# Attention backward on one core: K and V loads moved to the GpSimd queue, dO·O to VectorE, and nearly all K transposes to DMA

## The chip, the cores and the metric

The program runs on one core of one Trainium2 chip. Its engines work side by side, each through its own list of instructions in order: TensorE (PE, with its weight loads as PEld), VectorE (DVE), ScalarE (ACT), GpSimd (POOL) and SyncE (SP). SP does no arithmetic here; it issues DMAs. POOL computes and issues DMAs too, from a queue of its own. The metric is the device time of one execution in microseconds, given as the median of the runs; less is better.

## The reference

Two attention blocks A and B with the same shapes stand side by side. Each projects its input, attends to a cache of keys and values, and projects back; the two outputs are concatenated. The kernel computes the output and, for a given gradient of it, all ten gradients.

```python
B, Sq, D = 8, 96, 640
H, Sk, Dh = 32, 512, 128
def block(x, k_cache, v_cache, wq, wo):            # bfloat16
    q = (x @ wq).reshape(B, Sq, H, Dh).transpose(0, 2, 1, 3)
    s = einsum("bhqd,bhkd->bhqk", q, k_cache) * Dh ** -0.5
    p = softmax(s, axis=-1)
    o = einsum("bhqk,bhkd->bhqd", p, v_cache)
    return o.transpose(0, 2, 1, 3).reshape(B, Sq, H * Dh) @ wo
def forward(...):
    return concatenate([block(A...), block(B...)], axis=-1)
def reference(..., grad_out):
    out, vjp = jax.vjp(forward, A_x, ..., B_wo)
    return out, *vjp(grad_out)
```

## The kernel before

**Tiles and ticks.** One tile is one batch element of one head: 96 queries against 512 keys, with a head dimension of 128. There are 2 blocks x 32 heads x 8 batch elements = 512 tiles. They are worked in a software pipeline whose unit is a tick: tile number n stands at tick `ct = tick0 + h * 8 + b`, and each of its steps is given to an `Emitter` with a tick (`ct` plus an offset from the table `OFF`, line 45) and a slot within the tick (line 51). The emitter sorts by tick and slot and calls the steps (lines 21 to 28). A scheduler may then move instructions against this order. Those in `pinned(...)` (line 111) keep their program order, and those under `tc.high_priority` (the scores and the softmax, lines 291 to 331) move ahead.

**The steps of a tile**, with its tick offset. `c_ld` (line 262) loads K and V of two batch elements at once, 256 KB each: K at -5, V at -3, on SP. `c_xt` (line 272) is a crossbar DMA transpose on SP: VT, the transpose of a V pair, at 0 for all pairs, and KT at -3 for those K pairs that `k_on_pe` (line 548) does not send elsewhere. `c_s1` (line 280), at +2, transposes K on PE into `kT_ps`, four 128-column matmuls against the identity for each tile, and DVE copies the result to `KT_pe`. At +3 the scores follow, `S_ps = Q·KT` (line 298), their row maximum on DVE (`negm`, line 300), the exponential on ACT (`E_sb`, line 310), the reciprocal of the row sum on DVE (`rinv`, line 320), and the scaling on POOL (`P_sb`, line 329). At +4 PE transposes P (line 365) and computes dV (line 389); at +5 it computes O^T from V and P^T (line 359), and `c_s5b` (line 401) forms `prod = dO·O` on POOL. At +6 come dP = dO·VT (line 417), the row sums of `prod` (`dl_ps`, line 419) and dS on DVE (line 421); at +7 dK (line 432) and the transpose of dS (line 346); at +8 dQ^T from K (line 340). ACT evacuates O, dQ, P^T, dV and dK. Stores of dV and dK, two batch elements together (256 KB each), go out on POOL's queue in `c_st` (line 395), pinned, at slot 54.3.

**Where K is transposed before the change.** By line 549 on PE for every other pair of batch elements, for head 0 of both blocks and for head 1 of block A. That makes 268 tiles on PE; the other 244 tiles, 122 pairs, take a DMA.

**Buffers.** The pool `kv` holds 7 K pairs, 5 V pairs, 2 KT pairs and 4 VT pairs (lines 575 to 579). A load or transpose waits until the last reader of its buffer is done. All PSUM tiles share 8 banks.

**Work per head.** Beside its 8 tiles a head has projections and transposes of its own (pB, pC, pD, qA, qB, qD), put at fixed ticks around it. Heads form groups of 5 or 6 (2 at the end of B). When a group ends, `gU` (line 501) multiplies the group's O and dQ with the weights (`o_ps`, line 512), over some 14 to 18 ticks. So there are stretches of heads with this group work on PE and stretches without it.

**Queues.** SP's list in a steady stretch is the loads of K and V and the transposes KT and VT, each behind the waits of the one before. POOL's list in one tick is P_sb, prod, one store, and now and then a load of weights (`wq_p`, `wo_h`, lines 190 and 199) or a store of their gradients (lines 474 and 496).

Of the kernel before, what the change touches and what calls it, by code (L numbers as in the profile page):

```python
# [8 lines left out]
ALU = mybir.AluOpType  # L9
# [32 lines left out]
SL_GRP = 95  # L42
SL_SETUP = 96

OFF = dict(ldk=-5, ldv=-3, kt=-3, vt=0, s2=3, s3=3, s4=4, s5=5, s6=6, s7=7, s8=8)
HK = dict(pA=-10, pA2=-9, pB=-3, pC0=[-2, 0], pC1=[-1, 0], pD1=1, pD0=2, qA0=18, qA1=17, qB=[19, 20], qD=[(18, 0, 2), (19, 2, 4), (21, 4, 5)])
EV = dict(pB0="act", pB1="dve", pC00="act", pC01="act", pC10="act", pC11="dve", pD0="dve", pD1="dve", qA0="act", qA1="dve", qB0="act", qB1="dve", qD="dve", gU="act")
GSPREAD0 = 9
# [2 lines left out]
SLOTS = dict(LOAD=0, S2A=5, S2B=5.5, S1=6, S8=10, S7=20, S5=30, S4=40, S6=50, S3A=52, S3B=53, S5B=54, HEAD=SL_HEAD, GRP=SL_GRP)  # L51


def build_block(tc, em, tick0, blk, x, kc, vc, wq, wo, g_all, out_all, dx, dk, dv, dwq, dwo, ident, ones, pools, HG=6, first=True, groups=None):
    nc = tc.nc
# [7 lines left out]
    KC = Sk // 128  # L63
    NB = 2
# [46 lines left out]
    def pinned(ins):  # L111
        return tc.keep_in_program_order(ins)
# [68 lines left out]
    def pA(h):  # L181
        def f():
            start = first and h == 0
            if h % 2 == 0:
                wq_p = hd.tile([128, DC, 256], BF16, name="wq_p", bufs=2)
                with nc.allow_non_contiguous_dma(reason="wq slice of two heads"):
                    if start:
                        nc.sync.dma_start(wq_p[:], wq_v[:, :, h * 128:(h + 2) * 128])
                    else:
                        pinned(nc.gpsimd.dma_start(wq_p[:], wq_v[:, :, h * 128:(h + 2) * 128]))  # L190
            else:
                wq_p = HS[(blk, h - 1)]["wq_p"]
            HS[(blk, h)] = dict(wq_p=wq_p, wq_h=wq_p[:, :, (h % 2) * 128:(h % 2 + 1) * 128])
        return f

    def pA2(h):
        def f():
            wo_h = hst.tile([128, D], BF16, name="wo_h", bufs=HG + 3)
            ld = nc.gpsimd.dma_start(wo_h[:], wo[h * 128:(h + 1) * 128, :])
            if not (first and h == 0):  # L200
                pinned(ld)
            HS[(blk, h)]["wo_h"] = wo_h
        return f

    def pB(h):
        def f():
            st = HS[(blk, h)]
            woT_ps = bank([128, DC * 128], BF16, "woT_ps")
            for c in range(DC):
                nc.tensor.transpose(woT_ps[:, c * 128:(c + 1) * 128], st["wo_h"][:, c * 128:(c + 1) * 128], ident[:])  # L210
            woT_h = hd.tile([128, DC * 128], BF16, name="woT_h", bufs=1)
            evac(EV["pB0"], woT_h[:], woT_ps[:])
            st["woT_h"] = woT_h
            wqT_ps = bank([128, DC * 128], BF16, "wqT_ps")
            for c in range(DC):
                nc.tensor.transpose(wqT_ps[:, c * 128:(c + 1) * 128], st["wq_h"][:, c, :], ident[:])
            wqT_h = hst.tile([128, D], BF16, name="wqT_h")
            evac(EV["pB1"], wqT_h[:], wqT_ps[:])
            st["wqT_h"] = wqT_h
            st["slot"] = (blk * H + h) % OD.shape[2]  # L220
            st["OT_h"] = OD[:, 0, st["slot"]]
            st["dQT_h"] = OD[:, 1, st["slot"]]
            st["QT_h"] = hd.tile([128, T], BF16, name="QT_h")
            st["dOT_h"] = hd.tile([128, T], BF16, name="dOT_h")
        return f
# [36 lines left out]
    def c_ld(h, b, n, bufs):  # L262
        def f():
            src = kc if n == "K" else vc
            X = kvp.tile([128, NB, KC, 128], BF16, name=n + "_sb", bufs=bufs)
            nc.sync.dma_start(X[:], src[b:b + NB, h].rearrange("b (p c) d -> p b c d", c=KC))
            for i in range(NB):
                st = CS.setdefault((blk, h, b + i), {})
                st[n + "_sb"], st[n + "_all"] = X[:, i], X
        return f  # L270
# [130 lines left out]
    def c_s5b(h, b):  # L401
        def f():
            st = CS[(blk, h, b)]
            hs = HS[(blk, h)]
            tok = slice(b * Sq, (b + 1) * Sq)
            prod = wk.tile([128, Sq], BF16, name="prod", bufs=3)
            pinned(nc.gpsimd.tensor_tensor(prod[:], hs["OT_h"][:, tok], hs["dOT_h"][:, tok], op=ALU.mult))  # L407
            st["prod"] = prod
        return f

# [135 lines left out]
    NTS = len(tsplits)  # L546

    def k_on_pe(h, b):
        return (b // NB) % 2 == 0 or h == 0 or (first and h == 1)

    SX = pools["SX"]
    for g in range(NG):
        h0 = GH0[g]
        for hh in range(groups[g]):
            h = h0 + hh
            c0t = tick0 + h * B
            if not (first and h == 0):
                em.add(c0t + HK["pA"], 54.6, pA(h))
                em.add(c0t + HK["pA2"], 54.6, pA2(h))
            em.add(c0t + HK["pB"], SL_HEAD, pB(h))  # L560
            fh = first and h == 0
            p0, p1, d1, d0, late = HK["pC0"], HK["pC1"], HK["pD1"], HK["pD0"], 0
            if fh:
                p1, d1, d0, late = [3, 3], 3, 4, 7
            elif h == 0:
                p0, p1, d1, d0, late = [-2, 2], [0, 3], 3, 4, 7
            for si in range(NTS):
                em.add(c0t + p0[min(si, 1)], SL_HEAD, pC(h, 0, si))
                em.add(c0t + p1[min(si, 1)], SL_HEAD + late, pC(h, 1, si))
            em.add(c0t + d1, SL_HEAD + (8 if late else 0), pD(h, 1))  # L570
            em.add(c0t + d0, SL_HEAD, pD(h, 0))
            for b in range(B):
                ct = c0t + b
                if b % NB == 0:
                    em.add(tick0 - 12 if first and h == 0 and b == 0 else ct + OFF["ldk"], SLOTS["LOAD"], c_ld(h, b, "K", 7))
                    em.add(ct + OFF["ldv"], SLOTS["LOAD"], c_ld(h, b, "V", 5))
                    if not k_on_pe(h, b):
                        em.add(ct + OFF["kt"], SLOTS["LOAD"] + 1, c_xt(h, b, "KT", 2))
                    em.add(ct + OFF["vt"], SLOTS["LOAD"] + 1, c_xt(h, b, "VT", 4))
                if k_on_pe(h, b):  # L580
                    em.add(ct + 2, SLOTS["S1"], c_s1(h, b))
                em.add(ct + OFF["s2"], SLOTS["S2A"], c_s2a(h, b))
                em.add(ct + OFF["s2"], SLOTS["S2B"], c_s2b(h, b))
                em.add(ct + OFF["s3"], SLOTS["S3A"], c_s3a(h, b))
                em.add(ct + OFF["s3"], SLOTS["S3B"], c_s3b(h, b))
                em.add(ct + OFF["s5"], SLOTS["S5B"], c_s5b(h, b))
                if b % 2 == 1:
                    em.add(ct + OFF["s4"] + 1, 54.3, c_st(h, b, "v"))
                    em.add(ct + OFF["s7"] + 1, 54.3, c_st(h, b, "k"))
                em.add(ct + OFF["s4"], SLOTS["S4"], c_s4(h, b))  # L590
                for i, o in enumerate(("s8", "s7", "s5", "s4")):
                    SX.setdefault(ct + OFF[o], [None] * 4)[i] = (blk, h, b)
                em.add(ct + OFF["s6"], SLOTS["S6"], c_s6(h, b))
                em.add(ct + OFF["s7"], SLOTS["S7"], c_s7(h, b))
            hk = HK if first or h < H - 1 else dict(HK, qA0=13, qB=[14, 15], qA1=16, qD=[(19, 0, 2), (19, 2, 4), (19, 4, 5)])
            em.add(c0t + hk["qA0"], SL_HEAD, qA(h, 0))
            for di in range(len(wsplits)):
                em.add(c0t + hk["qB"][di], SL_HEAD + 1, qB(h, di))
            em.add(c0t + hk["qA1"], SL_HEAD, qA(h, 1))
            for (k_, c_lo, c_hi) in hk["qD"]:  # L600
                if c_lo < DC and h % 2 == 1:
                    em.add(c0t + k_, SL_HEAD + 2, qD(h, c_lo, min(c_hi, DC)))
        cLg = tick0 + (h0 + groups[g] - 1) * B + B - 1
        gs0 = max(3, (GSPREAD0 * groups[g]) // HG)
        gs1 = max(3, (GSPREAD1 * groups[g]) // HG)
        if not first and g == NG - 2:
            gs0, gs1 = 9, 9
        if g == 0:
            em.add(cLg + OFF["s5"] - 2, SL_LOAD, setup_acc)
        subs = [(0, t, gi) for t in range(TT) for gi in range(len(gsplits))] + [(1, t, gi) for t in range(TT) for gi in range(len(gsplits))]  # L610
        n_out = TT * len(gsplits)
        for i, (which, t, gi) in enumerate(subs):
            if which == 0:
                tk = cLg + OFF["s5"] + 2 + (i * gs0) // n_out
            else:
                tk = cLg + OFF["s8"] + 2 + gs0 - 3 + ((i - n_out) * gs1) // n_out
            em.add(tk, SL_GRP, gU(g, which, t, gi))
# [124 lines left out]
```

## Time and profile before

| | |
|---|---|
| median of 3 runs | 1707.16 us (1696.48 to 1713.74) |
| profiled execution, its span | 1699.8 us |
| mean granted TensorE clock | 0.998 |
| PEld, DVE, ACT, POOL busy | 79%, 78%, 83%, 61% of the span |
| DMA | 423.05 MB in 600429 packets, mean 249 GB/s |
| HBM read and written | 161.09 MB and 159.12 MB |

Busy time of an engine is the union of its instructions' spans. Instructions of PE and ACT overlap their followers, so a busy share near 100% on PE means that it is hardly ever empty, not that it is at its peak. The share of a DMA queue is the time of its packets over the time of 16 DMA engines; as packets overlap too, the shares may add up to more than 100%. In a group of instructions, the idle time is that of the engine just before it, with what ended it. The time to landing of a DMA runs from the start of its issue to its last completion.

### The profile page before, as it was taken

Reading aid. Unit: us, or ns where it says so; the run is one execution under the profiler, and the core shown is the slowest. Engines: PE = TensorE matmul, PEld = TensorE weight load, DVE = VectorE, ACT = ScalarE, POOL = GpSimd, SP = SyncE. Lnnn points to the kernel's source line nnn. Section 1 sums busy time; section 2 is a strip of 40 time slices with the busy share of each in tenths; the row PEclk is TensorE's granted clock in tenths of the full one; section 3 lists DMA queues with packets and bytes.
Section 4 is the critical chain, followed back from the end, with each engine's and each line's share of the span. In section 5 each row is a group of like instructions: output and inputs, shape, how many; then the busy total and the mean of one; then the engine's idle time right before and its main releaser. Section 6 shows DMA issues by size and latency. Waiting matters only on the chain.

```text
span 1699.8 us, 56567 instructions
## 1 busy us (share of the span) xinstructions
PE 1675.7 (99%) x22024; PEld 1343.8 (79%) x22024; DVE 1329.8 (78%) x3052; ACT 1405.2 (83%) x3518; POOL 1040.3 (61%) x1747
## 2 busy tenths in 40 slices
PE   8999999999999999999999999999999999999999
PEld 7877778778778778777778877887788778778876
DVE  6887678878788878787778876787788778878877
ACT  6998889869869869878768998897799679878975
POOL 3676567646647647656566764675576557656754
PEclk9999999999999999999999999999999999999999
DMA  9999999999999999999999999999899989999994
GB/s 256 252 259 250 258 225 260 262 242 243 262 221 252 268 238 259 225 251 237 281 256 269 273 270 248 238 289 248 218 261 276 237 221 261 281 217 240 263 247 141
DMA packets 600429, 423.05 MB, mean 249 GB/s; under 512 B 419360, under 2 KB 557984, under 8 KB 600160
## 3 DMA queue, kind: packets, MB, share of 16 engines
q1 hardware_dynamic: 546576, 242.08, 72.2%
q0 software_dynamic: 53584, 177.35, 32.7%
q8 instruction: 173, 2.83, 0.7%
q14 instruction: 96, 0.79, 0.2%
HBM read 161.09 MB, written 159.12 MB: 188 GB/s over the span
## 4 chain that ended last, share of the span: by engine, by line
PE 89%; DMA 4%; ACT 3%; issue 1%; DVE 1%; POOL 0%; SPq 0%; DVEq 0%; ACTq 0%; POOLq 0%
PE q_ps L243 12%; PE o_ps L512 12%; PE dwo_ps L470 6%; PE dV_ps L389 6%; PE dK_ps L432 6%; PE S_ps L298 6%; PE dP_ps L417 6%; PE dwq_ps L490 6%; PE x_ps L340 5%; PE x_ps L365 5%; PE dst_ps L346 5%; PE x_ps L359 5%; PE kT_ps L285 3%; PE n_ps L258 3%; PE nat_ps L455 2%; DMA VT<-V_sb 1%
## 5 line engine op out<-in xcount | busy, mean ns | idle before, releaser
L329 POOL TENSOR_SCALAR P_sb<-E_sb,rinv 96x512 bf16<-96x512 bf16 x512 | 352.6, 689 | 567.8 <-DVE rinv L320 559.2
L310 ACT ACTIVATE E_sb<-S_ps,negm 96x512 bf16<-96x512 f32 x512 | 351.0, 686 | 187.6 <-DVE negm L300 181.9
L421 DVE SCALAR_TENSOR_TENSOR dS_sb<-dP_ps,dl_ps,P_sb 96x512 bf16<-96x512 f32 x512 | 382.1, 746 | 60.9 <-PE dl_ps L419 54.6
L300 DVE TENSOR_REDUCE negm<-S_ps 96x1 f32<-96x512 f32 x512 | 347.6, 679 | 50.9 <-PE S_ps L298 46.6
L435 ACT ACTIVATE dK_sb<-dK_ps 128x512 bf16<-128x512 f32 x512 | 302.1, 590 | 63.4 <-PE dK_ps L432 56.5
L392 ACT ACTIVATE dV_sb<-dV_ps 128x512 bf16<-128x512 f32 x512 | 311.6, 609 | 0.0
L378 ACT ACTIVATE PT_sb<-x_ps 128x384 bf16<-128x384 bf16 x512 | 253.1, 494 | 0.0
L512 PEld LDWEIGHTS <-OD 128*128 128x128 bf16 x1536 | 132.2, 98 | 100.4 <-issue 1.0
L398 POOL DMA_DIRECT2D out_dram<-dV_sb x256 | 194.9, 761 | 11.8 <-issue 8.6
L398 POOL DMA_DIRECT2D out_dram<-dK_sb x256 | 195.0, 762 | 9.1 <-issue 4.4
L389 PE MATMUL dV_ps<-dOnat_h,P_sb 96*128 96x128 bf16 x2048 | 198.2, 219 | 0.8 <-DVE dOnat_h L160 0.6
L417 PE MATMUL dP_ps<-VT,dOT_h 128*96 128x512 bf16 x512 | 195.4, 382 | 3.0 <-DMA VT<-V_sb 3.0
L432 PE MATMUL dK_ps<-Qnat_h,dS_sb 96*128 96x128 bf16 x2048 | 198.1, 219 | 0.1
L407 POOL TENSOR_TENSOR prod<-OD,dOT_h 128x96 bf16<-128x96 bf16 x512 | 184.2, 360 | 13.8 <-ACT OD L375 12.6
L348 DVE COPY dST_sb<-dst_ps 128x384 bf16<-128x384 bf16 x512 | 177.1, 346 | 10.5 <-PE dst_ps L346 10.3
L365 PE MATMUL x_ps<-ident,P_sb 96*128 96x96 bf16 x2048 | 172.0, 205 | 0.8 <-POOL P_sb L329 0.3
L359 PE MATMUL x_ps<-PT_sb,V_sb 128*128 128x96 bf16 x2048 | 172.3, 206 | 0.2 <-ACT PT_sb L378 0.2
L346 PE MATMUL dst_ps<-ident,dS_sb 96*128 96x96 bf16 x2048 | 172.3, 206 | 0.2 <-DVE dS_sb L421 0.2
L340 PE MATMUL x_ps<-dST_sb,K_sb 128*128 128x96 bf16 x2048 | 171.0, 206 | 1.3 <-ACT dK_sb L435 0.8
L375 ACT ACTIVATE OD<-x_ps 128x192 bf16<-128x192 f32 (+1 forms) x515 | 167.9, 326 | 3.9 <-PE x_ps L340 3.9
L320 DVE RECIPROCAL rinv<-rowsum 96x1 f32<-96x1 f32 x512 | 79.9, 156 | 106.0 <-ACT E_sb L310 100.4
L340 PEld LDWEIGHTS <-K_sb 128*128 128x128 bf16 x2048 | 131.1, 98 | 25.1 <-issue 1.6
(84 smaller groups left out, 3744.4 us busy)
## 6 DMA issues: line engine op xcount, KB each, us to landing
out_dram<-dV_sb POOLq DMA_DIRECT2D x256, 256.0 KB, 5.2
out_dram<-dK_sb POOLq DMA_DIRECT2D x256, 256.0 KB, 5.3
K_sb<-in_A_k_cache_dram SPq DMA_DIRECT2D x128, 256.0 KB, 5.3
V_sb<-in_A_v_cache_dram SPq DMA_DIRECT2D x128, 256.0 KB, 5.2
K_sb<-in_B_k_cache_dram SPq DMA_DIRECT2D x128, 256.0 KB, 5.0
V_sb<-in_B_v_cache_dram SPq DMA_DIRECT2D x128, 256.0 KB, 4.9
out_dram<-dwo_sb POOLq DMA_DIRECT2D x63, 160.0 KB, 4.8
out_dram<-dwq_sb POOLq DMA_DIRECT2D x31, 320.0 KB, 6.1
```

The costliest lines, as they stand in the source:

```text
L300: nc.vector.tensor_reduce(negm[:], S_ps[:], axis=AX.X, op=ALU.max, negate=True)
L310: nc.scalar.activation(E_sb[:], st["S_ps"][:], ACT.Exp, bias=st["negm"][:], scale=1.0, accum_out=rowsum[:])
L329: pinned(nc.gpsimd.tensor_scalar(P_sb[:], st["E_sb"][:], st["rinv"][:], 0.0, op0=ALU.mult, op1=ALU.add))
L340: nc.tensor.matmul(dQT_ps, st["K_sb"][:, c, :], st["dST_sb"][:, c * Sq:(c + 1) * Sq], start=(c == 0), stop=(c == KC - 1))
L389: nc.tensor.matmul(dV_ps[:, c * 128:(c + 1) * 128], P_sb[:, c * 128:(c + 1) * 128], hs["dOnat_h"][:, b * 128:(b + 1) * 128], start=True, s ...
L392: nc.scalar.activation(SB[(blk, h, b // 2, "v")][:, b % 2], dV_ps[:], ACT.Identity, scale=1.0)
L398: pinned(nc.gpsimd.dma_start(dst[b - 1:b + 1, h].rearrange("b (p c) d -> p b (c d)", c=KC), SB.pop((blk, h, b // 2, which))[:]))
L417: nc.tensor.matmul(dP_ps[:], hs["dOT_h"][:, tok], st["VT"], start=True, stop=True)
L421: nc.vector.scalar_tensor_tensor(dS_sb[:], dP_ps[:], dl_ps[:, 0:1], st["P_sb"][:], op0=ALU.subtract, op1=ALU.mult)
L432: nc.tensor.matmul(dK_ps[:, c * 128:(c + 1) * 128], dS_sb[:, c * 128:(c + 1) * 128], hs["Qnat_h"][:, b * 128:(b + 1) * 128], start=True, s ...
L435: nc.scalar.activation(SB[(blk, h, b // 2, "k")][:, b % 2], dK_ps[:], ACT.Identity, scale=1.0)
L512: nc.tensor.matmul(o_ps[:], src[:, t * 128:(t + 1) * 128], rhs, start=(hh == 0), stop=(hh == groups[g] - 1))
```

## The change

Four edits, made together:

1. `c_ld` issues all loads of K and V from POOL's queue, pinned, but for head 0 of block A, which stays on SP. Their slot becomes 54.4, behind P_sb (53) and the stores (54.3) of the same tick, instead of 0.
2. V is loaded at tick -4 instead of -3.
3. `prod` is computed on DVE, not pinned, instead of POOL.
4. `k_on_pe` keeps PE transposes of K for head 0 of both blocks and head 1 of block A only. All other K pairs take a DMA transpose. The numbers of buffers stay as they are.

```diff
-OFF = dict(ldk=-5, ldv=-3, kt=-3, vt=0, s2=3, s3=3, s4=4, s5=5, s6=6, s7=7, s8=8)
+OFF = dict(ldk=-5, ldv=-4, kt=-3, vt=0, s2=3, s3=3, s4=4, s5=5, s6=6, s7=7, s8=8)
...
-            nc.sync.dma_start(X[:], src[b:b + NB, h].rearrange("b (p c) d -> p b c d", c=KC))
+            v = src[b:b + NB, h].rearrange("b (p c) d -> p b c d", c=KC)
+            if first and h == 0:
+                nc.sync.dma_start(X[:], v)
+            else:
+                pinned(nc.gpsimd.dma_start(X[:], v))
...
-            pinned(nc.gpsimd.tensor_tensor(prod[:], hs["OT_h"][:, tok], hs["dOT_h"][:, tok], op=ALU.mult))
+            (nc.vector.tensor_tensor(prod[:], hs["OT_h"][:, tok], hs["dOT_h"][:, tok], op=ALU.mult))
...
     def k_on_pe(h, b):
-        return (b // NB) % 2 == 0 or h == 0 or (first and h == 1)
+        return h == 0 or (first and h == 1)
...
-                    em.add(tick0 - 12 if first and h == 0 and b == 0 else ct + OFF["ldk"], SLOTS["LOAD"], c_ld(h, b, "K", 7))
-                    em.add(ct + OFF["ldv"], SLOTS["LOAD"], c_ld(h, b, "V", 5))
+                    sl = SLOTS["LOAD"] if first and h == 0 else 54.4
+                    em.add(tick0 - 12 if first and h == 0 and b == 0 else ct + OFF["ldk"], sl, c_ld(h, b, "K", 7))
+                    em.add(ct + OFF["ldv"], sl, c_ld(h, b, "V", 5))
```

## The prediction

> **What bounds the kernel now.** I read the page first for who is full, then DMA, then two-head stretches, then the orders on the queues. The page's busy times, queues, the GB/s of 40 slices, and the chain:
>
> ```profile
> PE 1675.7 (99%) x22024; PEld 1343.8 (79%) x22024; DVE 1329.8 (78%) x3052; ACT 1405.2 (83%) x3518; POOL 1040.3 (61%) x1747
> ...
> GB/s 256 252 259 250 258 225 260 262 242 243 262 221 252 268 238 259 225 251 237 281 256 269 273 270 248 238 289 248 218 261 276 237 221 261 281 217 240 263 247 141
> ...
> q1 hardware_dynamic: 546576, 242.08, 72.2%
> q0 software_dynamic: 53584, 177.35, 32.7%
> ...
> PE 89%; DMA 4%; ACT 3%; issue 1%; DVE 1%; POOL 0%; SPq 0%; DVEq 0%; ACTq 0%; POOLq 0%
> ```
>
> PE sets the time, but the DMA queues together are at 104.9% of 16 engines' packet time. The mean of these hides two kinds of stretch. In the answer by windows, the 45.2 us rows are two heads without group work ("light"), the others two heads with it ("heavy"); the columns are length, busy time of each engine, PE clock, DMA share, GB/s:
>
> ```profile
> 955.00:1000.20 45.20, 45.13 (x639) 37.81 (x636) 37.92 (x88) 42.72 (x109) 32.19 (x55) 1.00 1.16 267
> 1000.20:1061.10 60.90, 60.90 (x754) 46.49 (x751) 38.77 (x88) 51.14 (x129) 32.49 (x55) 1.00 1.07 260
> 1088.20:1133.40 45.20, 45.14 (x639) 37.81 (x637) 37.91 (x89) 42.73 (x109) 32.20 (x54) 1.00 1.10 274
> 1154.90:1216.40 61.50, 61.21 (x753) 46.61 (x751) 45.90 (x107) 44.45 (x111) 32.42 (x55) 1.00 0.98 237
> 1243.90:1289.10 45.20, 45.13 (x638) 37.81 (x636) 37.91 (x89) 42.72 (x109) 32.16 (x54) 1.00 1.10 263
> ```
>
> The light stretch takes the same 45.2 us each time: PE is bound there, ACT close behind at 42.7. Bytes of one head: loads 8 x 262 KB, stores 8 x 262 KB, transposes 4 VT and on average 2 KT, weights and their gradients 160 + 160 + (320 + 320)/2 KB, together 6.43 MB. Two heads in 45.2 us ask for 285 GB/s, and the windows moved 263 to 274; heavy ones ask for 211 and moved 237 to 260. So I read that DMA already falls behind in light stretches and catches up in heavy ones, unseen by PE because loads run ahead.
>
> **The change part by part.**
>
> *K off PE.* 268 tiles on PE become 24 (heads 0, 0 and 1), so 244 go. Cost of one, from the timeline of a light stretch (start, duration, engine, line):
>
> ```profile
> 1404.13 0.39 PE L285 MATMUL kT_ps<-ident,K_sb 128*128 128x128 bf16 x4
> ...
> 1404.35 0.33 PE L340 MATMUL x_ps<-dST_sb,K_sb 128*128 128x96 bf16 x4
> ```
>
> The next group starts 0.22 us later; the 0.39 is pipelined. 244 x 0.22 = 53.7 us off the path that sets the end (the chain gives line 285 3%, 51 us for 268, which agrees). That is 1.76 us per two heads: light 43.4, heavy about 59.4. With the copies DVE loses 244 x 0.41 = 100 us.
>
> *prod on DVE.* No row shows it there. Nearest from below the reciprocal on 96x1 (156 ns), from above an f32 addition on 128x128 out of PSUM (277 ns); I take 250, as the shape is nearest to the latter: 512 x 0.25 = 128 us (80 to 142). DVE ends near 1358 us, off the path. It waits for ACT's O in front of DVE's later work, but by the timeline that evacuation ends before dS, which precedes prod. A pause there would delay `negm`, on which ACT already waits 181.9 us. Cost 0, bounds -5 to +15.
>
> *Loads on POOL.* 504 of 512 loads move (block A's head 0 stays). The stores of equal size give the price:
>
> ```profile
> L398 POOL DMA_DIRECT2D out_dram<-dV_sb x256 | 194.9, 761 | 11.8 <-issue 8.6
> ...
> L407 POOL TENSOR_TENSOR prod<-OD,dOT_h 128x96 bf16<-128x96 bf16 x512 | 184.2, 360 | 13.8 <-ACT OD L375 12.6
> ```
>
> 504 x 0.761 = 384 us come, 184 us of prod go: POOL 1040 + 200 = 1240 us. In a light stretch 32.2 - 16 x 0.36 + 16 x 0.76 = 38.6 of 43.4 us. Each tick holds P_sb, one store, one load: the move of V to -4 puts K and V in alternate ticks, and costs nothing of its own; the fifth V buffer is free at that tick. Behind a load that waits stand the next P_sb and, for that, PE. A load waits for dQ or O matmuls early in its own tick, which are over, and in the built order each POOL DMA waits for the eighth before it, now 3.4 ticks (9 us) old instead of 7. Stores land in 5.2 us, at most 11.9, so this costs nothing until landing nears 9 us; bounds 0 to 40 us (P_sb up to 0.4 us late in 100 of the light ticks).
>
> On the price of issuing: the Trainium skill, "DMA: Bandwidth & Descriptors", Issuing engines are not separate DMA queues, says that all DMAs interleave on the same 16 engines and that spreading them saves sequencer time only. By that rule the move to POOL gives DMA no capacity, so it speaks against any gain there. The trace has the same work on both queues only at different packet sizes, so it can't confirm it.
>
> *122 more transposes.* 122 x 262 KB = 32 MB, 455 MB in all. SP has room: 504 issues leave. Price in DMA time, two ways.
> By bytes: four light windows (the three above, and one at 255) move 265 GB/s on average. 455 MB / 265 = 1717 us; at the best slice, 289, 1574.
> By packet time: q0 is 556 us for 177.35 MB, 3.13 us per MB; loads at the same price leave q1's 99 MB of transposes 1227 - 143 x 3.13 = 779 us, 2.06 us each. 122 more are 251 us, and the sum is 1783 + 251 = 2034 us of share. At 1.16, the fullest light window, that needs 1753 us; at 1.10, 1849.
> The trace doesn't show transposes beside loads on the software queue, whose packets are larger (177.35 MB in 53584 against 242.08 in 546576), so that the mixture could run better. I take the bytes, as the nearest measured thing, and the packet time for the upper end.
>
> The Trainium skill, "Advanced Engine Details and Errata", X-Bar Transpose (TRN2), holds transposes to be as fast as plain DMAs at 350 to 400 GB/s, which would make 122 of them an estimated 80 to 91 us. The landing times agree with it (KT 5.2 us, K 5.3); the 2.06 us of packet time each do not, and the measured row is taken.
>
> *KT buffers.* They stay at 2, sized for every second pair. Now a pair's transpose waits until the scores of the pair two before are done, and its own are due three ticks later. In the built order on SP, it also stands behind the VT of the same pair (1.25 us of issue). Landing:
>
> ```profile
> L275 SPq DMA_TRANSPOSE KT<-K_sb x122: 1231/1250/3126, 44.3 to 1647.3; - x122
> ...
> DMA to landing us min/median/max: 3.1/5.2/11.9
> ```
>
> Three light ticks are 3 x 2.7 = 8.1 us, less 0.2 for the scores and up to 1.25 for VT: 6.6 us against a median of 5.2. That cover is thin, and when it is gone PE itself waits.
>
> **Forecast: DMA sets the light stretches; slower.** After the change two light heads ask for 13.9 MB in 43.4 us, 320 GB/s; the fullest slice shows 289. Heavy ones ask for 234, so they gain, but can only take over what may be late: POOL's eight DMAs in flight (2.1 MB) and one transpose. PE's 53.7 us turn into waits of the scores for KT. The sum is 455 MB / 265 GB/s = 1717 us, plus the last slice, which cannot be filled (141 GB/s: (265 - 141)/265 x 42.5 = 20 us): span 1737. The median of the runs is 7.4 us over the profiled span, nothing else lies around it in the numbers shown: about 1740. Chance 0.45; its own range is 1710 to 1800 (rates of 269 to 255, or packet time).
>
> **Rival 1: PE keeps the time; faster.** Larger packets let DMA carry 277 GB/s on average (455 MB in 1646 us) and some 300 in light stretches. For it: the light windows lose nothing to DMA now, and slices of 276 to 289 exist. Against: no window holds 300. Then 1699.8 - 53.7 = 1646, plus some 5 for ticks where ACT (42.7 of 43.4) ends last, plus 7: 1658. It decides if KT lands within 6.6 us. Chance 0.30.
>
> **Rival 2: the two KT buffers alone; slower.** Aggregate DMA suffices, but store and load bursts delay each transpose to 8 us, as VT's (median 6.1, maximum 14.9) shows is possible. Then a tick is at least (8 + 1.25 + 0.4)/3 = 3.2 us, against 2.8 on average in light stretches now: 8 x 0.4 = 3.2 us for each of some 37 light heads (22.6 n + 30.6 (64 - n) = 1660), 118 us, less the 27 heavy heads' gain of 0.88: 1699.8 + 118 - 24 + 7 = 1801. It decides from a landing of about 6.6 us. Against: the pure median is 5.2. Chance 0.13.
>
> That the change doesn't do what it says is excluded: the built program has 244 KT transposes, 24 tiles left on PE, and prod on DVE. The remaining 0.12 is a mixture in which gain and waits cancel, between 1690 and 1724.
>
> **Numbers.** 1740; range 1655 to 1830, from rival 1 to the packet-time end. Within 1% (1690 to 1724) is about what a measurement of this kernel can tell from no change: 0.12, and 0.04 from the forecast's lower tail, make 0.16. Faster 0.30; slower 0.45 - 0.04 + 0.13 = 0.54.
>
> **What would show it.** Idle time of PE before `S_ps<-KT` put down to the DMA of KT, in light windows, tens of us in place of 2.1; KT landing over 6.6 us; light pairs over 45.2 us and heavy ones near 59.4; DMA over 265 GB/s there. Rival 2 is right if KT waits while GB/s stays under 260. Wrong altogether if light pairs come to 43.5 us with KT landing near 5, or if POOL's P_sb waits show POOL or DVE as the bound.

## The result, and the profile after

| | before | after |
|---|---|---|
| median of 4 runs each | 1703.21 us (1696.48 to 1713.74) | 2227.43 us (2214.36 to 2243.88) |
| ratio, 95% interval | | 1.306 (1.2974 to 1.3146): slower |
| span of the profiled run | 1699.8 us | 2231.7 us |
| granted TensorE clock | 0.998 | 0.891 |
| DMA | 423.05 MB, 249 GB/s | 454.90 MB, 204 GB/s |

The direction was forecast, the size was not: 2227 lies far over the range's upper end of 1830. The page of the changed kernel, with the lines for busy engines, GB/s of 40 slices, the two large queues (packets, MB, share of 16 engines) and the chain of waits by engine and by line:

```profile
PE 1774.5 (80%) x21048; PEld 1382.8 (62%) x21048; DVE 1338.0 (60%) x3320; ACT 1413.4 (63%) x3518; POOL 1224.8 (55%) x1739
...
GB/s 255 228 193 184 179 199 185 204 231 192 240 215 194 196 186 159 179 232 182 215 231 213 219 167 239 232 202 203 227 197 204 226 207 188 199 219 184 178 227 145
...
q1 hardware_dynamic: 538320, 141.92, 53.4%
q0 software_dynamic: 93904, 309.51, 53.0%
...
PE 48%; DMA 45%; DVE 3%; ACT 2%; issue 1%; SPq 0%; POOL 0%; DVEq 0%; ACTq 0%
DMA KT<-K_sb 44%; PE o_ps L516 8%; PE q_ps L243 5%; PE S_ps L302 4%; PE dwo_ps L474 4%; PE dwq_ps L494 3%; PE dK_ps L436 3%; PE dP_ps L421 3%; PE dV_ps L393 3%; PE dst_ps L350 3%; PE x_ps L344 3%; PE x_ps L369 2%; PE x_ps L363 2%; PE n_ps L258 1%; PE nat_ps L459 1%
```

PE is empty for a fifth of the span, and its place on the chain is taken by one thing, the DMA that brings KT: 44%. The GB/s line is the surprise. Only the first slice (255) holds what most slices held before; from the third on, most are near 200. The queues' shares add up to 106%, as before (105%): the DMA engines are as full of packet time as before, and move a fifth less.

The answer by windows, with two light stretches (three heads without group work each) and the two heavy heads that follow each (columns: length, busy time of each engine, PE clock, DMA share, GB/s):

```profile
309.00:428.40 119.40, 76.52 (x898) 60.24 (x896) 57.19 (x144) 64.25 (x161) 56.34 (x80) 0.83 1.11 183
428.40:487.90 59.50, 59.26 (x720) 44.76 (x718) 45.58 (x113) 44.14 (x110) 38.56 (x55) 1.00 1.03 235
1429.30:1537.00 107.70, 72.11 (x898) 58.15 (x895) 57.13 (x144) 64.02 (x161) 56.86 (x81) 0.84 1.13 195
1537.00:1596.50 59.50, 59.26 (x720) 44.75 (x717) 45.49 (x113) 43.95 (x110) 38.32 (x55) 1.00 1.15 234
```

The heavy pair takes 59.5 us, PE full, at 235 GB/s; its saving is there. A light head takes 36 to 40 us in place of 22.6, at 183 to 195 GB/s and with a DMA share of 1.11 to 1.13: DMA is always occupied and delivers less. The waits say who pays. Of the page's groups, the scores, with PE's idle time before them at the end of the line:

```profile
L302 PE MATMUL S_ps<-KT,QT_h 128*96 128x512 bf16 x488 | 207.4, 425 | 423.8 <-DMA KT<-K_sb 421.2
```

The same wait in the kernel before, in its answer on KT (us, times):

```profile
  DMA KT<-K_sb: 2.1, 1
```

In the answer for line 279, the issue of KT on SP (ns, min/median/max), and in the answer on DMA the median landing times (us):

```profile
L279 SPq DMA_TRANSPOSE KT<-K_sb x244: 1232/2499/8677, 42.5 to 2188.9; - x122
```

```profile
VT<-V_sb SPq DMA_TRANSPOSE x256, 6.3
KT<-K_sb SPq DMA_TRANSPOSE x244, 8.1
```

PE waits 421 us for KT, in place of 2.1. KT lands in 8.1 us at the median (5.2 before, 24.9 at most), and SP itself is held at the issue of a KT for 2.5 us in place of 1.25. By window the medians part: KT lands in 10.1 and 8.7 us in the two light stretches above, in 4.9 and 7.1 in the heavy pairs behind them.

**A measure for all runs.** The length of a head is taken from its first dV matmul to the next head's first. Heads 2 to 62 are 34 light and 27 heavy ones in every version. Their means, us:

| | light | heavy | span |
|---|---|---|---|
| before | 22.96 | 30.00 | 1699.8 |
| after | 36.65 | 32.42 | 2231.7 |

34 x 13.69 + 27 x 2.42 = 531 us, the whole difference of the spans (532). So the loss lies in the light heads to 465 us, and to 65 us in heavy ones, some of which wait too. Seen from PE, its empty time grows from 24 to 457 us, 433 of the 532. The other 99 us are busy time: PE takes longer over its matmuls (see the granted clock at the end), although 244 tiles of K have left it.

### The profile page after: what moved, and what is told of

Read it like the earlier page. It is cut to its first block, busy times and chain, and to the rows that moved or that the text cites. A ratio compares the mean times of both kernels' runs of the same rounds, so it can differ in the third digit from the quotient of the medians.

```text
span 2231.7 us, 54423 instructions
## 1 busy us (share of the span) xinstructions
PE 1774.5 (80%) x21048; PEld 1382.8 (62%) x21048; DVE 1338.0 (60%) x3320; ACT 1413.4 (63%) x3518; POOL 1224.8 (55%) x1739
## 2 busy tenths in 40 slices
DMA packets 632483, 454.90 MB, mean 204 GB/s; under 512 B 548192, under 2 KB 557792, under 8 KB 632224
## 3 DMA queue, kind: packets, MB, share of 16 engines
q1 hardware_dynamic: 538320, 141.92, 53.4%
q0 software_dynamic: 93904, 309.51, 53.0%
## 4 chain that ended last, share of the span: by engine, by line
PE 48%; DMA 45%; DVE 3%; ACT 2%; issue 1%; SPq 0%; POOL 0%; DVEq 0%; ACTq 0%
DMA KT<-K_sb 44%; PE o_ps L516 8%; PE q_ps L243 5%; PE S_ps L302 4%; PE dwo_ps L474 4%; PE dwq_ps L494 3%; PE dK_ps L436 3%; PE dP_ps L421 3%; PE dV_ps L393 3%; PE dst_ps L350 3%; PE x_ps L344 3%; PE x_ps L369 2%; PE x_ps L363 2%; PE n_ps L258 1%; PE nat_ps L459 1%
## 5 line engine op out<-in xcount | busy, mean ns | idle before, releaser
L302 PE MATMUL S_ps<-KT,QT_h 128*96 128x512 bf16 x488 | 207.4, 425 | 423.8 <-DMA KT<-K_sb 421.2
L302 PEld LDWEIGHTS <-QT_h 128*96 128x96 bf16 x512 | 65.8, 129 | 463.3 <-DMA KT<-K_sb 448.2
L436 PE MATMUL dK_ps<-Qnat_h,dS_sb 96*128 96x128 bf16 x2048 | 212.0, 230 | 0.0
L393 PE MATMUL dV_ps<-dOnat_h,P_sb 96*128 96x128 bf16 x2048 | 210.5, 229 | 0.6 <-DVE dOnat_h L160 0.6
L421 PE MATMUL dP_ps<-VT,dOT_h 128*96 128x512 bf16 x512 | 207.4, 405 | 0.8 <-DVE dOnat_h L160 0.8
L369 PE MATMUL x_ps<-ident,P_sb 96*128 96x96 bf16 x2048 | 182.0, 213 | 5.1 <-POOL P_sb L333 4.8
L350 PE MATMUL dst_ps<-ident,dS_sb 96*128 96x96 bf16 x2048 | 183.1, 215 | 2.8 <-DVE dS_sb L425 1.6
L363 PE MATMUL x_ps<-PT_sb,V_sb 128*128 128x96 bf16 x2048 | 183.1, 214 | 0.1
L344 PE MATMUL x_ps<-dST_sb,K_sb 128*128 128x96 bf16 x2048 | 183.1, 216 | 0.1
L344 PEld LDWEIGHTS <-K_sb 128*128 128x128 bf16 x2048 | 146.3, 104 | 45.3 <-issue 4.1
```

Source lines behind the costliest of these rows:

```text
L302: nc.tensor.matmul(S_ps[:], hs["QT_h"][:, tok], st["KT"], start=True, stop=True)
L344: nc.tensor.matmul(dQT_ps, st["K_sb"][:, c, :], st["dST_sb"][:, c * Sq:(c + 1) * Sq], start=(c == 0), stop=(c == KC - 1))
L393: nc.tensor.matmul(dV_ps[:, c * 128:(c + 1) * 128], P_sb[:, c * 128:(c + 1) * 128], hs["dOnat_h"][:, b * 128:(b + 1) * 128], start=True, s ...
L436: nc.tensor.matmul(dK_ps[:, c * 128:(c + 1) * 128], dS_sb[:, c * 128:(c + 1) * 128], hs["Qnat_h"][:, b * 128:(b + 1) * 128], start=True, s ...
```

## The experiments

The theory after the result: crossbar transposes on SP's hardware queue, beside loads on POOL's software queue, lower what DMA moves. The rivals: two KT buffers; the number of transposes; the software queue by itself; 256-byte pieces of one queue beside another; prod on DVE.

**Loads back on SP, all else as changed** (e1_loads_sp; V at -3 and the loads in their old slot again)

```diff
-            if first and h == 0:
-                nc.sync.dma_start(X[:], v)
-            else:
-                pinned(nc.gpsimd.dma_start(X[:], v))
+            nc.sync.dma_start(X[:], v)
```

> The changed kernel with all K and V loads back on SP (V at tick -3); nearly all K still transposed by DMA, two KT buffers, prod on DVE. Theory M (mixture: transposes on the hardware queue beside loads on the software queue lower what DMA carries, so KT lands late): DMA back near 250 GB/s, KT landing near 6 us, waits for KT below 100 us, time 1700 to 1790. Theory B (two KT buffers: a transpose is due three ticks after its buffer comes free, whichever queue loads use): waits for KT stay above 300 us, time above 2000.

1820.71 us, ratio 1.0693 (1.0606 to 1.0779). The theory's rate came true; its time (up to 1790) and its waits (under 100 us) were both passed by a little. The scores' group on its page:

```profile
L299 PE MATMUL S_ps<-KT,QT_h 128*96 128x512 bf16 x488 | 193.2, 396 | 110.8 <-DMA KT<-K_sb 106.0
```

Windows of a light stretch of three heads, and of two heavy heads:

```profile
1249.60:1309.10 59.50, 59.26 (x720) 44.75 (x718) 45.64 (x113) 44.04 (x110) 26.58 (x38) 1.00 1.05 235
1336.60:1413.80 77.20, 69.57 (x900) 56.19 (x897) 56.39 (x144) 63.77 (x161) 39.18 (x57) 0.96 1.17 261
1672.80:1751.40 78.60, 68.84 (x898) 55.56 (x896) 56.67 (x144) 63.75 (x161) 39.91 (x57) 0.96 1.14 267
```

The same bytes, the same 500 transposes, the same two KT buffers, and DMA moves 253 to 267 GB/s in five light stretches, two of them shown. So 407 of the 524 us lost hang on the queue of the loads, with what goes along with it: on SP's hardware queue the trace records a load in packets of 1024 bytes, on POOL's software queue in packets of 4096. No run here parts the queue from the size of its packets. What remains, 117 us, is a light head of 26.80 us; heavy ones take 29.93.

**Every other K pair back on PE, loads on POOL** (e2_k_alt)

```diff
-        return h == 0 or (first and h == 1)
+        return (b // NB) % 2 == 0 or h == 0 or (first and h == 1)
```

> The changed kernel with every other K pair back on PE (k_on_pe as before); loads on POOL, V at -4, prod on DVE. Theory M: 378 transposes beside the same loads on the software queue still slow DMA: below 230 GB/s, time 1800 to 2000. Theory B: with every second pair the two buffers have seven ticks, no wait for KT: 1690 to 1730.

2543.78 us, ratio 1.4939 (1.4833 to 1.5045): with 122 transposes fewer it is the slowest of all, slower too than the 1800 to 2000 of the theory. The page, then the answer for line 279:

```profile
GB/s 254 200 203 147 154 172 173 157 153 174 166 195 171 155 131 143 158 154 175 238 219 181 166 149 172 148 168 156 135 157 136 156 166 166 166 148 147 166 154 164
...
q0 software_dynamic: 93904, 309.51, 58.9%
q1 hardware_dynamic: 409488, 109.92, 54.3%
```

```profile
L279 SPq DMA_TRANSPOSE KT<-K_sb x122: 1232/5318/12092, 48.4 to 2480.8; - x122
...
DMA to landing us min/median/max: 3.3/19.3/29.0
```

The number of transposes is not the price. 110 MB on the hardware queue now take more packet time (54.3% of 2529.1 us, 1373) than 142 MB did in the changed kernel (53.4% of 2231.7 us, 1192), and the median transpose, K's or V's, lands after 19.3 us.

**Four KT buffers** (e3_kt4; one buffer of another pool, `stp`, given up for the room)

```diff
-                        em.add(ct + OFF["kt"], SLOTS["LOAD"] + 1, c_xt(h, b, "KT", 2))
+                        em.add(ct + OFF["kt"], SLOTS["LOAD"] + 1, c_xt(h, b, "KT", 4))
...
-            stp=P(name="stp", bufs=5),
+            stp=P(name="stp", bufs=4),
```

> The changed kernel with four KT buffers for two, and four for five small staging buffers to make room. Theory M: DMA stays near 200 GB/s, since the buffers alter nothing of what it carries; the waits move to another operand: time above 2050. Theory B: the transposes run ahead, PE waits for KT under 30 us, DMA at 270 GB/s, time 1650 to 1700.

2387.61 us in the profiled run (2458.13 in a second), slower than every run of the changed kernel (2243.88 at most). The answer on DMA of the profiled run, median landing in us:

```profile
VT<-V_sb SPq DMA_TRANSPOSE x256, 11.1
KT<-K_sb SPq DMA_TRANSPOSE x244, 12.0
```

More buffers, and each transpose lands later (12.0 against 8.1 us), at 191 GB/s against 204 over the run. The theory expected the waits to move to another operand; but 401.6 us of them still are for KT, and 77.7 for VT have come. So more buffers don't cure the loss. Two look like a brake on it, as they keep fewer transposes under way; e2 fits that, where KT's two buffers serve half as many pairs. The traces agree as far as they go: the times from issue to landing of all transposes, divided by the span, give 2.0 under way on average in the changed kernel, 2.6 in e3 and 2.7 in e2 (1.7 in e1, 1.4 before). But this number also grows when each lands later, so it remains an argument. The effect of one `stp` buffer was not measured apart.

**prod on DVE alone** (e4_prod_dve: the kernel before with this one edit)

```diff
-            pinned(nc.gpsimd.tensor_tensor(prod[:], hs["OT_h"][:, tok], hs["dOT_h"][:, tok], op=ALU.mult))
+            (nc.vector.tensor_tensor(prod[:], hs["OT_h"][:, tok], hs["dOT_h"][:, tok], op=ALU.mult))
```

> The kernel before with prod on DVE alone. Both theories: within 0.5% of before, 1695 to 1715; if prod on DVE holds up negm or P_sb (POOL waited 126 us for prod in the changed kernel), above 1720.

1721.92 us, ratio 1.0108 (1.0071 to 1.0144). Its page, the chain and the group:

```profile
PE 66%; ACT 12%; DVE 10%; issue 6%; DMA 4%; POOL 1%; ACTq 0%; SPq 0%; DVEq 0%; POOLq 0%
...
L408 DVE TENSOR_TENSOR prod<-OD,dOT_h 128x96 bf16<-128x96 bf16 x512 | 133.2, 260 | 38.3 <-ACT OD L376 38.3
```

260 ns each, as estimated (250). But DVE now stands idle for 38.3 us at `prod`, until ACT has evacuated O, and the chain runs through ACT and DVE for 22% in place of 4%. Light heads take 23.36 us in place of 22.96, heavy ones 30.46 in place of 30.00: a small price on every tick. Here DVE still copies all of PE's K; in the whole change it doesn't.

**No transposes at all, loads on POOL, and on SP** (x3_no_transpose: e2 without; x6_no_transpose_sp: e4 without)

```diff
-            XT = kvp.tile([128, NB * KC, 128], BF16, name=name, bufs=bufs)
-            nc.sync.dma_start_transpose(XT[:], CS[(blk, h, b)][name[0] + "_all"][:].rearrange("p a c d -> p (a c d)"))
+            X = CS[(blk, h, b)][name[0] + "_all"]
...
-                CS[(blk, h, b + i)][name] = XT[:, i * KC:(i + 1) * KC].rearrange("p c k -> p (c k)")
+                CS[(blk, h, b + i)][name] = X[:, i].rearrange("p c d -> p (c d)")
```

> The kernel of e2 without any DMA transpose: it leaves out the transposes of V and K by DMA and reads V and K themselves in their place. The 309 MB on the software queue stay. If transposes beside that queue are what slows DMA: landing of loads and stores near 4 us, no DMA waits on PE, time 1700 to 1740 (that of e4, 1722). If the software queue is slow by itself with loads and stores on it: landing stays above 10 us, time above 2000.

> The kernel of e4 (loads on SP) without DMA transposes: it leaves out the transposing of V and K and reads them as they are. Against x3 (1742), which has the loads on POOL, it gives the price of issuing from POOL without any transposes. If that is nothing but POOL's time: 1715 to 1745, x3 within 1.5% of it.

x3: 1742.31 us in one run (before 1706.95 beside it). x6: 1715.3 us, ratio 1.0071 (1.0037 to 1.0104). From e2 to x3 some 800 us go with the transposes, so the software queue alone costs little. x3 is 27 us slower than x6, and a wait that this edit makes can account for it, since V itself is now held until dP and POOL's list stops at its load; PE then waits 19.5 us for P_sb (1.3 in e4). The waits of x3:

```profile
POOL V_sb L270 <- PE dl_ps L422: 264.9, 145, 4.3
```

But leaving them out leaves out their bytes as well (324 MB, 186 GB/s). The next pair keeps the bytes.

**Plain copies in place of the transposes** (x4_copy256: e2 with them; x5_copy256_sp: e4 with them). The same 256 KB by the same queue from and to the same places, in 256-byte pieces; the target's rows are 144 long so that the pieces stay apart, and the matmuls read 128 of them.

```diff
-            XT = kvp.tile([128, NB * KC, 128], BF16, name=name, bufs=bufs)
-            nc.sync.dma_start_transpose(XT[:], CS[(blk, h, b)][name[0] + "_all"][:].rearrange("p a c d -> p (a c d)"))
+            XT = kvp.tile([128, NB * KC, 144], BF16, name=name, bufs=bufs)
+            nc.sync.dma_start(XT[:, :, 0:128], CS[(blk, h, b)][name[0] + "_all"][:].rearrange("p a c d -> p (a c) d"))
```

> The kernel of e2 (loads on POOL) with each DMA transpose replaced by a plain copy of the same 256 KB from SBUF to SBUF on SP, in 1024 pieces of 256 bytes: it leaves out the transposing of V and K and uses them as they are. Theory P (small packets of one queue take turns with the 4 KB packets of the other): DMA under 200 GB/s, landing of the copies above 12 us, time above 2000, as e2. Theory X (it is peculiar to transposes): copies land in about 5 us, time near x3 (1740).

> The same plain copies of 256 byte pieces in the kernel of e4 (loads on SP, in the queue of the copies). Both theories: near e4, 1715 to 1750, copies land in 4 to 6 us; it shows how far the copies stand for the transposes.

x4: 1712.51 us in one run, x5: 1712.42 in one, before 1704.69 beside both. The page of x4, against that of e2 above:

```profile
GB/s 256 274 284 273 196 238 277 254 199 260 262 198 288 265 201 273 265 206 287 264 272 272 282 259 205 253 283 219 225 263 281 211 223 283 263 198 249 281 210 138
...
q0 software_dynamic: 93904, 309.51, 54.4%
q1 hardware_dynamic: 403440, 109.90, 28.7%
```

Same queues, same bytes, packets within 2%, and 2544 us become 1712. The 1373 us of packet time on the hardware queue become 491 (28.7% of 1710.5 us). So neither small pieces nor two queues at once cost this; it is the transposing of the crossbar. And with plain copies the loads' queue makes no difference in this pair (1712 both).

**The change whole, and e1, with plain copies** (x7_copy256_after, x8_copy256_e1; the edit of x4 on the changed kernel and on e1)

> The changed kernel whole (loads on POOL, V at -4, prod on DVE, 244 KT and 256 VT moves, two KT buffers), but each crossbar transpose is a plain copy on SP with the same bytes in the same 256-byte pieces (left out: the transposing of K and V, so scores and dP are of other numbers). Theory (crossbar transposes beside loads of another queue are the whole loss): the rest of the change then shows PE's saving of 53.7 us against the 18.7 us that prod on DVE cost alone: between 1650 and 1690, DMA at 265 GB/s or more (455 MB in that time), KT landing at 4 to 5 us. Rival (two KT buffers, or loads on POOL's instruction list, cost of their own): over 1720, with waits of the scores for KT over 50 us or of P_sb for POOL. Second rival (the sum of bytes is the limit, whatever the form): at 249 GB/s, 1827.

> As e1_loads_sp (loads back on SP, K of nearly all heads through a DMA, prod on DVE, two KT buffers), with plain copies in 256-byte pieces in place of the transposes (left out: the transposing of K and V). If e1_loads_sp's 6.9% come of the crossbar's own price in DMA time: 1650 to 1700, with hardly any wait for KT. If they come of the two KT buffers or of the sum of bytes: 1780 or more again, with waits of the scores for KT near the 106 us there.

x7: 1709.94 us, ratio 1.0031 (0.9992 to 1.0069). x8: 1684.98 us, ratio 0.9895 (0.9825 to 0.9966). The scores' group on the page of x7, with the same two KT buffers and the same 244 transfers into them as in the changed kernel:

```profile
L302 PE MATMUL S_ps<-KT,QT_h 128*96 128x512 bf16 x488 | 186.3, 382 | 24.5 <-DMA KT<-K_sb 22.2
```

Windows of x8: a heavy pair, a light stretch of three heads, and two single heads of it:

```profile
1145.10:1204.60 59.50, 58.70 (x707) 44.73 (x717) 45.18 (x113) 44.24 (x111) 27.07 (x39) 1.00 0.86 247
1231.20:1297.80 66.60, 65.39 (x895) 53.77 (x896) 55.29 (x144) 62.86 (x161) 39.18 (x57) 1.00 1.06 305
1231.20:1252.40 21.20, 21.09 (x294) 17.33 (x293) 18.06 (x49) 20.34 (x53) 12.63 (x19) 1.00 1.05 296
1252.40:1276.50 24.10, 23.11 (x311) 19.00 (x312) 19.07 (x48) 22.09 (x58) 13.88 (x20) 1.00 1.08 320
```

Without the crossbar DMA moves 300 to 307 GB/s in light stretches of the same three heads that e1 carries at 253 to 267. x7 missed the theory's 1650 to 1690 and the rival's 1720 alike. The reason is in the table: the heavy heads give 0.6 to 0.8 us each, the light ones nothing.

| us | light | heavy | span | light stretches, GB/s |
|---|---|---|---|---|
| before | 22.96 | 30.00 | 1699.8 | 255 to 274 |
| e1, loads on SP | 26.80 | 29.93 | 1829.6 | 253 to 267 |
| after | 36.65 | 32.42 | 2231.7 | 183 to 196 |
| x8, e1 with copies | 23.09 | 29.18 | 1683.0 | 300 to 307 |
| x7, after with copies | 23.40 | 29.39 | 1699.3 | 293 to 308 |

In x8 light heads come in turn at 21.3 us, with PE full, and at some 24.5 us, those with most of the matmuls of `dwq_ps`, where PE works for 23.1. On the chain of the latter of the two heads above, this piece, with its start and length:

```profile
1262.11 8.39 DMA KT<-K_sb
```

So in this head even a plain copy of K ends last, at 320 GB/s; PE waits 0.7 us for it. In x7, the loads on POOL cost 16 us of span over x8 (34 x 0.31 + 27 x 0.21); the copies of K land in 5.8 us there, in 5.3 in x8.

**Not tried:** the loads on a second hardware queue, or in other packets on the same one, which would part the queue from the size of its packets; the stores moved to SP in exchange for the loads, which would part both from the amount on the software queue (309.51 MB after, 177.35 before); four KT buffers with the loads on SP, which is where a version faster than the kernel before might lie. None of the versions run that computes all of the reference beats it. Whether e1's last 117 us are, beside prod on DVE, the crossbar's pace alone or also the two KT buffers at a landing of 6.3 us is left open: x8 with the same two buffers waits 13.1 us for KT (e1: 106.0), but its copies land sooner (5.3).

## Why the prediction was right in direction and wrong in size

**What held.** K off PE: 0.88 us for each heavy head was forecast. The undisturbed heavy pair takes 59.5 us (forecast 59.4), and x8's heavy heads are 0.82 shorter. In light heads it brought nothing, even in x8 (23.09 against 22.96, with prod on DVE in it). That light stretches, not heavy ones, decide, and that the scores waiting for KT would show it: 421 us of them, and 44% of the chain. POOL's total was forecast at 1240 us and is 1224.8, DVE's at 1358 and is 1338.0. The move of the loads gave DMA no capacity, as the Trainium skill, "DMA: Bandwidth & Descriptors", Issuing engines are not separate DMA queues, has it. That such a move could take capacity away, that section doesn't say, and 2227 against 1821 us shows it.

**The step that failed first: the rate.** The prediction divided by 265 GB/s, "I take the bytes, as the nearest measured thing", for a mixture that "the trace doesn't show", and allowed only "that the mixture could run better". It ran at 183 to 196 GB/s in light stretches. The runs name the condition: transposes on the hardware queue beside loads on the software queue, in the packets that it makes of them. Take away either the transposing (x7: 1710) or the loads from that queue (e1: 1821), and the rate is back. The packet time failed with the bytes: the prediction kept each packet's price and came to 2034 us of it on the two queues, and the changed kernel spent 106.4% of 2231.7 us, 2375. An unseen mixture needed a bound below the measured rate as well as above it, and neither the bytes nor the packet time gave one.

**The second: the sum over the whole span.** "455 MB / 265 GB/s = 1717" lets heavy stretches run at 265 too, although the same prediction says that they ask for 234 and can take over little. In e1, where the rate did hold (253 to 267), the sum has to be made by stage: a light pair of 13.9 MB at 265 is 52.5 us, a light head 26.2. Then 34 x (26.2 - 22.96) - 27 x 0.88 = 86 us on 1699.8, and 7 beside the span: 1793, against 1820.71 measured with a light head of 26.80. The prediction had the parts of this sum, and lost 53 us by the mean.

**Rival 2, two KT buffers: its sign in the profile appeared, its cause and price didn't.** "KT waits while GB/s stays under 260" came true to the letter, and even its landing of 8 us (8.1 at the median). But its 1801 took 8 us for every light tick. The KT issued in light heads land in 11.4 us in the mean, and with that its own rule, (11.4 + 1.25 + 0.4)/3, gives 4.35 us a tick, 34.8 a head against 36.65 measured. So the two buffers fit as the way by which a late KT becomes time on PE; what makes it late is DMA's rate, which this rival took to be sufficient. With copies the same two buffers cost 22.2 us of waiting (x7), and four with transposes made it worse (2387.61). The sign didn't tell a transpose that waits for a buffer from one that DMA carries slowly; the landing time, counted from the issue, does. SP's issue time doesn't: 2.4 us at the median in e1, 2.5 after.

**Rival 1, PE keeps the time:** it asked for some 300 GB/s in light stretches. Plain copies reach that and still give 1685, not 1658. The waits for KT that are left there, 13.1 us, are a part of this difference. The rest is not shown; prod on DVE, 18.7 us when measured alone, is the nearest candidate.

**prod on DVE:** cost 0, bounds -5 to +15; measured alone 1721.92 - 1703.27 = 18.7 us. That "by the timeline that evacuation ends before dS" did not hold on 98 of the 512 ticks, where DVE waits for O.

**Equal speed of transpose and copy.** The landing times of before agreed with the Trainium skill's statement ("Advanced Engine Details and Errata", X-Bar Transpose (TRN2)) that a transpose is as fast as a plain DMA. Beside other work it isn't, here: e1 against x8 is 136 us for 500 transposes, 0.27 us of time each, and e2 against x4 is 831 us for 378. The prediction was right to prefer the measured packet time to it, but used it for the upper end only, and at a fixed price.

## What to carry to other kernels

A DMA rate read from a trace belongs to that mixture of queues and kinds: before moving a transfer to another queue, ask what it will then run beside, and bound the rate of an unseen mixture from below too. Make the sum by stage, where each stage's demand stands against the rate, since a mean over stages lets the slack of one pay for another. And where a wait for a buffer and a slow transfer look alike, a run with more buffers helps to tell them apart.

## What the runs showed of the hardware

Crossbar transposes from SBUF to SBUF on the hardware queue, beside loads on the software queue, brought DMA from 249 GB/s to 204 (two KT buffers), 191 (four) and 167 (half of K). The records of single packets show it on both queues: a transpose's 256-byte packet takes 31.3 ns in the mean before, 35.7 after and 54.6 in e2, where 13.7% take over 100 ns (1.9% before). Its median is 18 ns in all three, so it is a few long packets that cost the time; as a plain copy in x4 it takes 18.8 in the mean. The 4096-byte packets of the software queue go from 204 ns to 249 and, in e2, 314. Why is open: no run here looks into the crossbar, nor varies the software queue's packets.

Where PE waits, its granted clock is lower: 0.83 and 0.84 in the light windows of after and 1.00 in the heavy ones beside them, 0.92 to 0.96 in those of e1 and 1.00 in x8's. The score matmul, right behind the waits, takes 425 ns in the mean after and 382 in x7, with a median of 379 in both.
